# Attention and FFN in chunks of 512 tokens in place of 384

## The chip, the core and the metric

The kernel runs on one core of one Trainium2 chip. A core has five engines that run their own instruction streams in order: PE (TensorE, matrix multiply), DVE (VectorE), ACT (ScalarE), POOL (GpSimd) and SP (SyncE, which here only issues DMAs). They meet at semaphores. PE writes its results to PSUM, eight banks of 512 fp32 columns by 128 partitions; everything else lies in SBUF or in DRAM.

The metric is device time in microseconds. The kernel before takes 1013.74 us, the median of three runs (1013.64 to 1013.81).

## The reference

Windowed causal attention on 8 batches, 8 heads, 576 tokens and head size 64, then a feed-forward net with a rational function between its two products:

```python
scores = (1 / sqrt(64)) * q @ k.T              # window of 64: 0 <= i - j < 64
attn   = softmax(where(mask, scores, -1e9))
x      = (attn @ v)                            # to 4608 tokens x 512
h = x @ w_in                                   # 512 -> 2048
P = a[0] + a[1]*h + a[2]*h**2 + a[3]*h**3
Q = 1 + abs(b[0])*abs(h) + abs(b[1])*h**2
out = (P / (Q + 1e-6)) @ w_out                 # 2048 -> 512
```

## The kernel before

**Tiling.** The 4608 tokens are cut into 12 chunks of CH = 384. A chunk's attention is done in four *units*, one per pair of heads (`unit_load`, `unit_scores`, `unit_transpose`, `unit_av`). A unit leaves x transposed, 128 channels by CH tokens, split into a high part `xh` and a low part `xl`. The FFN goes through 16 tiles of 128 hidden channels; a *step* is one chunk and one such tile. `ffn1(c, i)` is 12 matmuls (four channel blocks, three products of high and low parts) into one bank `h` of CH columns, and then the rational function on ACT, DVE and POOL, which leaves `gh` and `gl`. `ffn2(s)` multiplies these with a tile of w_out: three matmuls of 512 columns for each 128 tokens, added up over a chunk's 16 steps in one output bank per 128 tokens (`o0` to `o2`).

**The rational function.** ACT reads h three times as absolute value and as two linear terms (L265 to L267); DVE continues the numerator (L268, L269); POOL multiplies u by |h| (L270); ACT takes logarithm and exponential of that (L273, L274), which together are the reciprocal; DVE forms gh and gl (L275 to L278). POOL stands between L267 and L273, and DVE behind L274.

**The attention unit.** PE writes the scores to the two banks `ps_s`; DVE adds the mask and takes the row maximum (L211, L214; in chunks 1 and 2 PE adds the mask, and only the maximum is left, L207); ACT takes exponentials with row sums (L221, L218); DVE makes reciprocals (L223, L224); POOL multiplies (L225; DVE in chunk 0); PE transposes into the same two banks (L232); ACT copies to `pT` (L234); PE multiplies with v into the bank `ps_x` (L243); ACT and DVE split that into xh and xl (L248, L249).

**Weights.** All weights stay in SBUF in a high and a low part. They arrive as 64-bit numbers and are decoded in 32 tiles: ACT (L124, L132), POOL (L127) and DVE (L128, L129, L133).

**Order.** `phases` lists the steps: chunks 0 and 1 go through the first eight hidden tiles, then both through the last eight, and then every chunk through all 16. So weights of the second half are needed only from step 16. Chunk 0's partial sums are put aside in SBUF between its two halves. FFN2 lags LAG = 3 steps behind FFN1 in the text of the program; the units of the next chunk begin AHEAD = 3 steps before the current chunk does. The text's order is not the engines' order: a scheduler with a model of the durations of its own places each engine's instructions when the program is built, within what data, buffers and banks allow. What buffers allow is set by the pools: PSUM has two banks for h, two for ps_s, one for ps_x and three for o.

Of the kernel before, what the change touches and what calls it, by code (L numbers as in the profile page):

```python
# [30 lines left out]
def swa_rational_ffn(ctx: ExitStack, tc: tile.TileContext, qT, kT, v, w_in, w_out, a, b, out):  # L31
# [71 lines left out]

    wi_h = const.tile([P, NCC, DFF], F32R, name="wi_h")
    wi_l = const.tile([P, NCC, DFF], F32R, name="wi_l")
    wo_h = const.tile([P, NF, DO], F32R, name="wo_h")
    wo_l = const.tile([P, NF, DO], F32R, name="wo_l")
# [45 lines left out]
    def unit_load(c, hp):  # L153
        q = kv.tile([P, TC, WIN], F32, name="q")
        kt = kv.tile([P, TC + 1, WIN], F32, name="kt")
        vt = kv.tile([P, TC, P], F32, name="vt")
# [20 lines left out]

        m0 = None if first is None else MASKS[first]
        live[c, hp] = dict(q=q, kt=kt, vt=vt, kw=kw, vw=vw, m0=m0)

    def unit_scores(c, hp):
        u = live[c, hp]

        ps = ps_a.tile([P, 2, 512], F32, name="ps_s", bufs=1)
# [9 lines left out]
        for p in range(PR):  # L194
            for z in range(2):
                for e in range(2):
# [8 lines left out]
        if on_pe:
# [3 lines left out]
        else:  # L209
# [4 lines left out]
            nc.vector.tensor_reduce(out=nmx, in_=sm, axis=AX.X, op=ALU.max, negate=True)  # L214
        sums = att.tile([P, NR], F32, name="sums")
        for j in range(NR):
# [3 lines left out]
            else:  # L220
                nc.scalar.activation(sm[:, j, :], sm[:, j, :], AF.Exp, bias=nmx[:, j:j + 1], accum_out=sums[:, j:j + 1])  # L221
# [6 lines left out]
    def unit_transpose(c, hp):  # L228
        u = live[c, hp]
        ps = ps_a.tile([P, 2, 512], F32, name="ps_s", bufs=1)  # L230
        for j in range(2 * PR):
            nc.tensor.transpose(ps[:, j // PR, (j % PR) * P:(j % PR + 1) * P], u["sm"][:, j, :], ident)  # L232
# [1 line left out]
        nc.scalar.copy(out=pT, in_=ps[:, :, 0:PR * P])  # L234
# [18 lines left out]
    def ffn1(c, i):  # L253
        h = ps_h.tile([P, CH], F32, name="h")
        n = 0
        for cc in range(NCC):
            for w, x in ((wi_h, xl), (wi_h, xh), (wi_l, xh)):
                nc.tensor.matmul(h, w[:, cc, i * P:(i + 1) * P], x[c, cc], start=n == 0, stop=n == 3 * NCC - 1)  # L258
                n += 1
# [28 lines left out]
    def ffn2(s):  # L288
# [3 lines left out]
        if first:  # L292
            acc[c] = [ps_o.tile([P, DO], F32, name=f"o{t}") for t in range(NTS)]
        gh, gl = gs.pop((c, i))
        for t in range(NTS):
            ts = slice(t * P, (t + 1) * P)
            for n, (g, w) in enumerate(((gl, wo_h), (gh, wo_l), (gh, wo_h))):
                nc.tensor.matmul(acc[c][t], g[:, ts], w[:, i, :], start=first and n == 0, stop=last and n == 2)  # L298
        if not last:
            return  # L300
        o = acc.pop(c)
        if c == 0 and c not in part:
# [4 lines left out]
        for t in range(NTS):
            ob = part[0][:, t, :] if s == total - 1 else stage.tile([P, DO], F32, name="ob", tag="w_st", bufs=3)
            if c in part:
                nc.vector.tensor_tensor(out=ob, in0=o[t], in1=part[c][:, t, :], op=ALU.add)  # L310
            else:
                nc.scalar.copy(out=ob, in_=o[t])
# [96 lines left out]
```

## Time and profile before

| | |
|---|---|
| median of three runs | 1013.74 us |
| the profiled execution (known by its span) | 1014.7 us |
| busy in the span: PE, DVE, ACT, POOL | 954.8, 825.9, 725.1, 324.9 us |
| matmuls of FFN1 (L258), 384 columns | 3 x 768 |
| matmuls of FFN2 (L298), 512 columns | 3 x 576 |
| mean granted clock of PE | 0.971 of full speed |

A row of a timeline has the start in us from the span's start, the duration, engine, line, operation, output and inputs, shapes and count, and in brackets how long the engine had been idle and what ended that. A matmul's duration is longer than the distance to the next one, since matmuls overlap; what one costs PE is the distance. A row of the groups has, behind the shapes, count, busy time in us, mean ns of one, and the idle time before them with what ended it. PE stands for matmuls, PEld for loads of the stationary operand, which overlap.

### The profile page before, as it was taken

How to read it: one execution, taken by the hardware profiler on the slowest of the kernel's cores; microseconds unless marked ns; L12 is line 12 of the kernel's file. 1: busy time of each engine (PE TensorE's matmuls, PEld its weight loads, DVE VectorE, ACT ScalarE, POOL GpSimd, SP SyncE). 2: the span in 40 equal slices, each digit the busy share in tenths (PEclk: the TensorE clock that was granted, in tenths of full speed). 3: DMA queues.
4: the chain of work that ended last, by engine and by line, in shares of the span. 5: the costliest groups of instructions: out<-in, count | busy, mean ns of one | idle time of the engine just before them, and what ended most of it. 6: DMA issues, size and time to landing. Idle time of an engine off the chain costs nothing.

```text
span 1014.7 us, 18277 instructions
## 1 busy us (share of the span) xinstructions
PE 954.8 (94%) x6640; PEld 844.8 (83%) x6640; DVE 825.9 (81%) x1539; ACT 725.1 (71%) x1735; POOL 324.9 (32%) x283
## 2 busy tenths in 40 slices
PE   3688578999999999999999999999999999999997
PEld 2576367989898888898888888888988988988996
DVE  7899788878888788788788787787787888787885
ACT  5777666667676777877777777777777777777664
POOL 4566544223332222223223223223223223222221
PEclk9679789999999999999999999999999999999999
DMA  7634630021211211210211211110121111100000
GB/s 239 221 110 138 207 98 16 1 77 29 90 31 31 83 42 34 88 37 29 76 46 31 67 58 34 64 61 29 61 61 31 62 63 35 64 17 1 32 1 31
DMA packets 37817, 64.09 MB, mean 63 GB/s; under 512 B 4448, under 2 KB 24928, under 8 KB 37728
## 3 DMA queue, kind: packets, MB, share of 16 engines
q1 hardware_dynamic: 37728, 62.93, 19.4%
q8 instruction: 52, 0.85, 0.4%
q14 instruction: 37, 0.30, 0.1%
HBM read 53.48 MB, written 9.44 MB: 62 GB/s over the span
## 4 chain that ended last, share of the span: by engine, by line
PE 84%; DVE 10%; ACT 3%; issue 2%; POOL 1%; DMA 1%; SPq 0%; POOLq 0%; DVEq 0%
PE h L258 38%; PE o L298 37%; PE ps_x L243 3%; PE ps_s L200 3%; PE ps_s L232 3%; DVE w_c L128 2%; POOL w_st L127 1%; DVE w_c L129 1%; DVE wo_l L133 1%; DVE num L277 1%; DVE u L276 1%; DVE wi_l L133 1%; DVE gh L275 1%; DMA w_st<-w_in 1%; ACT w_c L124 0%
## 5 line engine op out<-in xcount | busy, mean ns | idle before, releaser
L270 POOL TENSOR_TENSOR u<-u,ah 128x384 f32<-128x384 f32 x192 | 198.2, 1033 | 383.3 <-ACT u L267 343.7
L258 PE MATMUL h<-xl,wi_h 128*128 128x384 f32 x768 | 267.5, 348 | 20.3 <-DVE num L269 18.6
L258 PE MATMUL h<-xh,wi_h 128*128 128x384 f32 x768 | 262.7, 342 | 0.0
L258 PE MATMUL h<-xh,wi_l 128*128 128x384 f32 x768 | 262.5, 342 | 0.0
L298 PE MATMUL o<-wo_h,gl 128*128 128x512 f32 x576 | 233.5, 405 | 7.2 <-DVE gl L278 7.2
L298 PE MATMUL o<-wo_h,gh 128*128 128x512 f32 x576 | 228.3, 396 | 0.0
L298 PE MATMUL o<-wo_l,gh 128*128 128x512 f32 x576 | 227.0, 394 | 0.0
L268 DVE TENSOR_TENSOR num<-num,h 128x384 f32<-128x384 f32 x192 | 106.2, 554 | 111.9 <-ACT num L266 111.5
L265 ACT ACTIVATE ah<-h 128x384 f32<-128x384 f32 x192 | 94.5, 492 | 124.1 <-PE h L258 84.9
L258 PEld LDWEIGHTS h<-xl,wi_h 128*128 128x128 f32 x768 | 147.3, 192 | 27.8 <-DVE num L269 20.7
L258 PEld LDWEIGHTS h<-xh,wi_h 128*128 128x128 f32 x768 | 147.4, 192 | 4.8
L225 POOL TENSOR_TENSOR sm<-sm,rs 128x768 f32<-128x768 f32 x44 | 68.4, 1555 | 253.2 <-DVE rs L224 250.5
L258 PEld LDWEIGHTS h<-xh,wi_l 128*128 128x128 f32 x768 | 147.0, 191 | 0.6 <-issue 0.2
L275 DVE SCALAR_TENSOR_TENSOR gh<-num,a_sb,ah 128x384 fp32r<-128x384 f32 x192 | 119.3, 633 | 28.4 <-ACT ah L274 28.3
L298 PEld LDWEIGHTS o<-wo_h,gl 128*128 128x128 f32 x576 | 109.0, 189 | 33.7 <-DVE gl L278 8.8
L267 ACT ACTIVATE u<-ah,b_sb 128x384 f32<-128x384 f32 x192 | 135.6, 707 | 0.0
L221 ACT ACTIVATE sm<-sm,nmx 128x128 f32<-128x128 f32 x240 | 93.3, 390 | 57.4 <-DVE nmx L214 57.4
L298 PEld LDWEIGHTS o<-wo_h,gh 128*128 128x128 f32 x576 | 109.3, 190 | 25.2
L266 ACT ACTIVATE num<-h,a_sb 128x384 f32<-128x384 f32 x192 | 128.3, 668 | 0.0
L298 PEld LDWEIGHTS o<-wo_l,gh 128*128 128x128 f32 x576 | 109.2, 190 | 18.5
L269 DVE SCALAR_TENSOR_TENSOR num<-num,a_sb,h 128x384 f32<-128x384 f32 x192 | 117.7, 614 | 6.1
L277 DVE SCALAR_TENSOR_TENSOR num<-num,a_sb,u 128x384 f32<-128x384 f32 x192 | 116.7, 622 | 0.4
(52 smaller groups left out, 1139.2 us busy)
## 6 DMA issues: line engine op xcount, KB each, us to landing
out<-ob SPq DMA_DIRECT2D x33, 256.0 KB, 2.5
w_st<-w_in SPq DMA_DIRECT2D x16, 512.0 KB, 3.7
w_st<-w_out SPq DMA_DIRECT2D x16, 512.0 KB, 4.2
q<-qT SPq DMA_DIRECT2D x32, 192.0 KB, 3.2
vt<-v SPq DMA_DIRECT2D x16, 384.0 KB, 3.1
vt<-v SPq DMA_DIRECT2D x16, 320.0 KB, 3.0
kt<-kT SPq DMA_DIRECT2D x16, 224.0 KB, 3.6
kt<-kT SPq DMA_DIRECT2D x16, 192.0 KB, 3.4
```

The source lines that it names most:

```text
L221: nc.scalar.activation(sm[:, j, :], sm[:, j, :], AF.Exp, bias=nmx[:, j:j + 1], accum_out=sums[:, j:j + 1])
L225: (nc.vector if c < 1 else nc.gpsimd).tensor_tensor(out=sm, in0=sm, in1=rs.unsqueeze(2).broadcast_to([P, NR, P]), op=ALU.mult)
L258: nc.tensor.matmul(h, w[:, cc, i * P:(i + 1) * P], x[c, cc], start=n == 0, stop=n == 3 * NCC - 1)
L265: nc.scalar.activation(ah, h, AF.Abs)
L266: nc.scalar.activation(num, h, AF.Identity, scale=a_sb[:, 3:4], bias=a_sb[:, 2:3])
L267: nc.scalar.activation(u, ah, AF.Identity, scale=b_sb[:, 1:2], bias=b_sb[:, 0:1])
L268: nc.vector.tensor_tensor(out=num, in0=num, in1=h, op=ALU.mult)
L269: nc.vector.scalar_tensor_tensor(out=num, in0=num, scalar=a_sb[:, 1:2], in1=h, op0=ALU.add, op1=ALU.mult)
L270: nc.gpsimd.tensor_tensor(out=u, in0=u, in1=ah, op=ALU.mult)
L275: nc.vector.scalar_tensor_tensor(out=gh, in0=num, scalar=a_sb[:, 0:1], in1=ah, op0=ALU.add, op1=ALU.mult)
L277: nc.vector.scalar_tensor_tensor(out=num, in0=num, scalar=a_sb[:, 0:1], in1=u, op0=ALU.add, op1=ALU.subtract)
L298: nc.tensor.matmul(acc[c][t], g[:, ts], w[:, i, :], start=first and n == 0, stop=last and n == 2)
```

## The change

A chunk has 512 tokens, so there are nine. FFN1's matmuls and everything on h are 512 columns wide; a unit's scores, transposes and copies have eight blocks of 128 in place of six. An output chunk has four blocks of 128 tokens, held as two tiles of two banks each (`o0`, `o1`). To make room in PSUM, AV's result `ps_x` loses its own bank and takes turns with h in the two banks of `ps_h`; the scores of chunk 0 use the output banks. In SBUF, FFN2 lags two steps, the attention pools have one buffer, q and v of later chunks share the staging buffers of the weights, chunk 0's partial sums go to DRAM and come back, and the buffers of the attention of chunks 0 and 1 are given up at step SWITCH = 7 to the weights of the last eight tiles. The cut diff:

```diff
-CH = 384
+CH = 512
 TC = CH // WIN
 PR = TC // 2
 AHEAD = 3
-LAG = 3
+SWITCH = 7
+LAG = 2
...
-    kv = ctx.enter_context(tc.tile_pool(name="kv", bufs=2))
-    att = ctx.enter_context(tc.tile_pool(name="att", bufs=2))
+    kv = ctx.enter_context(tc.tile_pool(name="kv", bufs=1))
+    att = ctx.enter_context(tc.tile_pool(name="att", bufs=1))
...
+    early = ExitStack()
+    ekv = early.enter_context(tc.tile_pool(name="ekv", bufs=4))
+    eatt = early.enter_context(tc.tile_pool(name="eatt", bufs=2))
     ps_h = ctx.enter_context(tc.tile_pool(name="ps_h", bufs=2, space=bass.MemoryType.PSUM))
-    ps_a = ctx.enter_context(tc.tile_pool(name="ps_a", bufs=3, space=bass.MemoryType.PSUM))
+    ps_a = ctx.enter_context(tc.tile_pool(name="ps_a", bufs=1, space=bass.MemoryType.PSUM))
     ps_o = ctx.enter_context(tc.tile_pool(name="ps_o", bufs=1, space=bass.MemoryType.PSUM))
...
+    def weights(pool, tiles):
+        for i in tiles:
+            for d, n in (wi_h, "wi_h"), (wi_l, "wi_l"):
+                d[i] = pool.tile([P, NCC, P], F32R, name=f"{n}{i}")
+            for d, n in (wo_h, "wo_h"), (wo_l, "wo_l"):
+                d[i] = pool.tile([P, DO], F32R, name=f"{n}{i}")
+
+    weights(const, range(H))
...
+        if c < 2:
+            q = ekv.tile([P, TC, WIN], F32, name="q")
+            kt = ekv.tile([P, TC + 1, WIN], F32, name="kt")
+            vt = ekv.tile([P, TC - 1, P], F32, name="vt")
+        else:
+            q = stage.tile([P, TC, WIN], F32, name="q", tag="w_c")
+            kt = kv.tile([P, TC + 2, WIN], F32, name="kt")
+            vt = stage.tile([P, TC, P], F32, name="vt", tag="w_st", bufs=3)
...
+    def scores_bank(c, hp):
+        if c:
+            return ps_a.tile([P, 2, 512], F32, name="ps_s")
+        return ps_o.tile([P, 2, DO], F32, name="ps_s", tag=f"o{hp % 2}")
...
-        ps = ps_a.tile([P, TC, WIN], F32, name="ps_x", bufs=1)
+        ps = ps_h.tile([P, TC, WIN], F32, name="ps_x", tag="h")
...
-            acc[c] = [ps_o.tile([P, DO], F32, name=f"o{t}") for t in range(NTS)]
+            pair = [ps_o.tile([P, 2, DO], F32, name=f"o{t}") for t in range(NTS // 2)]
+            acc[c] = [pair[t // 2][:, t % 2, :] for t in range(NTS)]
...
-            part[c] = const.tile([P, NTS, DO], F32, name="part")
+            part[c] = []
             for t in range(NTS):
-                nc.scalar.copy(out=part[c][:, t, :], in_=o[t])
+                ob = stage.tile([P, DO], F32, name="ob", tag="w_st", bufs=3)
+                nc.scalar.copy(out=ob, in_=o[t])
+                part[c].append(tc.dram_tile([P, DO], F32, name=f"part{t}"))
+                nc.sync.dma_start(out=part[c][t], in_=ob)
             return
...
             if c in part:
-                nc.vector.tensor_tensor(out=ob, in0=o[t], in1=part[c][:, t, :], op=ALU.add)
+                nc.sync.dma_start(out=ob, in_=part[c][t])
+                nc.vector.tensor_tensor(out=ob, in0=o[t], in1=ob, op=ALU.add)
...
     for s in range(total + LAG):
+        if s == SWITCH:
+            early.close()
+            weights(ctx.enter_context(tc.tile_pool(name="late", bufs=1, reuse_waits="tile")), range(H, NF))
```

The scheduler makes other orders of it. Lines move too: L265 to L278 are L286 to L299 in the change, L221, L223, L224 are L242, L244, L245, L232, L234, L243 are L253, L255, L264, and L298 is L319. Three places from the middle of the program follow, one unit of a late chunk each.

PE before, where a unit's transposes (`ps_s<-ident,sm`) stand; xl and xh are FFN1's inputs, o is an output bank:

```order
L298 MATMUL o_2698<-wo_h,gh 128x512
L232 MATMUL ps_s<-ident,sm 128x128 x6
L258 MATMUL h<-xl_2428,wi_h 128x384
L258 MATMUL h<-xh_2427,wi_h 128x384
L258 MATMUL h<-xh_2427,wi_l 128x384
L258 MATMUL h<-xl_2645,wi_h 128x384
```

PE now, at the same place:

```order
L319 MATMUL o_5021<-wo_h_1187,gh 128x512
L253 MATMUL ps_s<-ident,sm 128x128 x8
L264 MATMUL ps_x<-pT,vt 64x64 x16
L279 MATMUL h<-xl_3771,wi_h_1193 128x512
L279 MATMUL h<-xh_3770,wi_h_1193 128x512
L279 MATMUL h<-xh_3770,wi_l_1194 128x512
```

Before, 24 matmuls of FFN1 (two steps) stand between the transposes and AV (`ps_x<-pT,vt`), which needs the copy pT of their result; now AV stands right behind them. It is so in 27 of the 28 units of chunks 2 to 8.

ACT before, from one unit's copy pT to the next step pair (ah, num and u belong to the step whose h they read):

```order
L234 COPY pT_3967<-ps_s_3960 128x768
L265 ACTIVATE ah_4086<-h_4073 128x384
L266 ACTIVATE num_4088<-h_4073,a_sb_87 128x384
L267 ACTIVATE u_4087<-ah_4086,b_sb_89 128x384
L265 ACTIVATE ah_4160<-h_4147 128x384
L266 ACTIVATE num_4162<-h_4147,a_sb_87 128x384
L267 ACTIVATE u_4161<-ah_4160,b_sb_89 128x384
L273 ACTIVATE ah_4086<-u_4087 128x384
L248 CAST xh3_3982<-ps_x_3969 128x384
L274 ACTIVATE ah_4086<-ah_4086 128x384
L273 ACTIVATE ah_4160<-u_4161 128x384
L274 ACTIVATE ah_4160<-ah_4160 128x384
```

ACT now, from one unit's copy on:

```order
L255 COPY pT_4497<-ps_s_4488 128x1024
L269 CAST xh3_4516<-ps_x_4499 128x512
L286 ACTIVATE ah_4545<-h_4532 128x512
L287 ACTIVATE num_4547<-h_4532,a_sb_93 128x512
L288 ACTIVATE u_4546<-ah_4545,b_sb_95 128x512
L294 ACTIVATE ah_4545<-u_4546 128x512
L295 ACTIVATE ah_4545<-ah_4545 128x512
L286 ACTIVATE ah_4587<-h_4574 128x512
L287 ACTIVATE num_4589<-h_4574,a_sb_93 128x512
L288 ACTIVATE u_4588<-ah_4587,b_sb_95 128x512
L294 ACTIVATE ah_4587<-u_4588 128x512
L295 ACTIVATE ah_4587<-ah_4587 128x512
```

Before, the first three operations of two steps stand together, and the logarithms behind both; now each step is finished before the next is opened. A third step of the same form follows, then the unit's eight exponentials, a fourth step and the next copy pT. At a chunk's end the four copies to the output buffers stand among these: two before the last operation of the step ahead of the eight exponentials, two around the start of the step behind them.

DVE before, where a unit's row sums (`sums`) stand against gl:

```order
L277 SCALAR_TENSOR_TENSOR num_4088<-num_4088,a_sb_87,u_4087 128x384
L277 SCALAR_TENSOR_TENSOR num_4162<-num_4162,a_sb_87,u_4161 128x384
L278 TENSOR_TENSOR gl_4090<-num_4088,ah_4086 128x384
L278 TENSOR_TENSOR gl_4164<-num_4162,ah_4160 128x384
L223 SCALAR_TENSOR_TENSOR sums_4127<-sums_4127,zero_126 128x6
L224 RECIPROCAL rs_4134<-sums_4127 128x6
```

DVE now, where the third step's gl is made:

```order
L296 SCALAR_TENSOR_TENSOR gh_4632<-num_4631,a_sb_93,ah_4629 128x512
L297 SCALAR_TENSOR_TENSOR u_4630<-u_4630,gh_4632 128x512
L244 SCALAR_TENSOR_TENSOR sums_4677<-sums_4677,zero_132 128x8
L298 SCALAR_TENSOR_TENSOR num_4631<-num_4631,a_sb_93,u_4630 128x512
L245 RECIPROCAL rs_4686<-sums_4677 128x8
L299 TENSOR_TENSOR gl_4633<-num_4631,ah_4629 128x512
```

The row sums, which need all eight exponentials, stood behind both gl; now they stand ahead of the last two operations that make one.

More of the change, by code (lines that the diff above doesn't have):

```diff
@@ L40, in swa_rational_ffn @@
     NCH = NTOK // CH
+    H = NF // 2
     NTS = CH // P
@@ L79, in make_mask @@
         nc.vector.tensor_copy(out=mask, in_=raw[:, 0:1, :].broadcast_to([P, NM, P]))
-        for j, half in FIRST.items():
+        for half, j in enumerate(KIND):
             hs = slice(half * 64, half * 64 + 64)
@@ L101, in swa_rational_ffn @@
     nc.vector.memset(zero, 0.0)
[L104 to L107, printed above, removed]
+    wi_h, wi_l, wo_h, wo_l = {}, {}, {}, {}
+    def weights(pool, tiles):
[5 more added lines that the diff above has]
+    weights(const, range(H))
     w_out_v = w_out.rearrange("(fc p) e -> p fc e", p=P)
@@ L135, in load_w_in @@
     def load_w_in(i):
-        sl = slice(i * P, (i + 1) * P)
-        decode(w_in[i], wi_h[:, :, sl], wi_l[:, :, sl])
+        decode(w_in[i], wi_h[i], wi_l[i])
     def load_w_out(i):
-        decode(w_out_v[:, i, :], wo_h[:, i, :], wo_l[:, i, :])
+        decode(w_out_v[:, i, :], wo_h[i], wo_l[i])
     xh, xl = {}, {}
@@ L153, in unit_load @@
     def unit_load(c, hp):
-        q = kv.tile([P, TC, WIN], F32, name="q")
-        kt = kv.tile([P, TC + 1, WIN], F32, name="kt")
-        vt = kv.tile([P, TC, P], F32, name="vt")
+        if c < 2:
[6 more added lines that the diff above has]
+            vt = stage.tile([P, TC, P], F32, name="vt", tag="w_st", bufs=3)
         kw, vw, first = [], [], None
@@ L176, in unit_load @@
             vb += nw
-        m0 = None if first is None else MASKS[first]
+        m0 = None if first is None else KIND[first % 2] - first // 2
         live[c, hp] = dict(q=q, kt=kt, vt=vt, kw=kw, vw=vw, m0=m0)
+    def scores_bank(c, hp):
+        if c:
+            return ps_a.tile([P, 2, 512], F32, name="ps_s")
+        return ps_o.tile([P, 2, DO], F32, name="ps_s", tag=f"o{hp % 2}")
     def unit_scores(c, hp):
         u = live[c, hp]
-        ps = ps_a.tile([P, 2, 512], F32, name="ps_s", bufs=1)
+        pool = eatt if c < 2 else att
+        ps = scores_bank(c, hp)
         m0 = u["m0"]
@@ L201, in unit_scores @@
                                      k[:, w:w + P], start=not on_pe, stop=not on_pe or p == PR - 1)
-        sm = att.tile([P, 2 * PR, P], F32, name="sm")
+        sm = pool.tile([P, 2 * PR, P], F32, name="sm")
         NR = 2 * PR
-        nmx = att.tile([P, NR], F32, name="nmx")
+        nmx = pool.tile([P, NR], F32, name="nmx")
         if on_pe:
@@ L214, in unit_scores @@
             nc.vector.tensor_reduce(out=nmx, in_=sm, axis=AX.X, op=ALU.max, negate=True)
-        sums = att.tile([P, NR], F32, name="sums")
+        sums = pool.tile([P, NR], F32, name="sums")
         for j in range(NR):
@@ L221, in unit_scores @@
                 nc.scalar.activation(sm[:, j, :], sm[:, j, :], AF.Exp, bias=nmx[:, j:j + 1], accum_out=sums[:, j:j + 1])
-        rs = att.tile([P, NR], F32, name="rs")
+        rs = pool.tile([P, NR], F32, name="rs")
         nc.vector.scalar_tensor_tensor(out=sums, in0=sums, scalar=1e-9, in1=zero, op0=ALU.add, op1=ALU.add)
@@ L229, in unit_transpose @@
         u = live[c, hp]
-        ps = ps_a.tile([P, 2, 512], F32, name="ps_s", bufs=1)
+        ps = ps_a.tile([P, 2, 512], F32, name="ps_s")
         for j in range(2 * PR):
             nc.tensor.transpose(ps[:, j // PR, (j % PR) * P:(j % PR + 1) * P], u["sm"][:, j, :], ident)
-        pT = att.tile([P, 2, PR * P], F32, name="pT", bufs=1)
+        pT = (eatt if c < 2 else att).tile([P, 2, PR * P], F32, name="pT")
         nc.scalar.copy(out=pT, in_=ps[:, :, 0:PR * P])
@@ L257, in ffn1 @@
             for w, x in ((wi_h, xl), (wi_h, xh), (wi_l, xh)):
-                nc.tensor.matmul(h, w[:, cc, i * P:(i + 1) * P], x[c, cc], start=n == 0, stop=n == 3 * NCC - 1)
+                nc.tensor.matmul(h, w[i][:, cc, :], x[c, cc], start=n == 0, stop=n == 3 * NCC - 1)
                 n += 1
@@ L297, in ffn2 @@
             for n, (g, w) in enumerate(((gl, wo_h), (gh, wo_l), (gh, wo_h))):
-                nc.tensor.matmul(acc[c][t], g[:, ts], w[:, i, :], start=first and n == 0, stop=last and n == 2)
+                nc.tensor.matmul(acc[c][t], g[:, ts], w[i], start=first and n == 0, stop=last and n == 2)
         if not last:
```

12 lines of the change are left out of this document (5 added, 7 removed).

## Prediction

> **What bounds the kernel now.** I read the page's head first, then the busy time by stretches of time, then the chain of work that ended last, then the timelines of the four engines over one attention unit.
>
> ```profile
> span 1014.7 us, 18277 instructions
> PE   3688578999999999999999999999999999999997
> 0.00:212.70 212.70, 158.63 (x1103) 135.49 (x1104) 184.15 (x310) 142.31 (x348) 101.69 (x79) 0.87 0.40 125
> 0.00:253.50 253.50, 199.43 (x1389) 171.52 (x1390) 215.84 (x372) 172.25 (x422) 112.90 (x89) 0.89 0.36 114
> 500.00:1000.00 500.00, 500.00 (x3447) 447.32 (x3446) 403.60 (x772) 364.50 (x858) 139.33 (x128) 1.00 0.13 42
> ```
>
> The columns of the stretches are length, busy PE, weight loads, DVE, ACT, POOL, granted clock, DMA share, GB/s. There are two regimes. From about 175 us on PE has no gap. Before that it is idle a quarter of the time, and DVE, busy 184.15 of the first 212.7 us, leads: it decodes 32 weight tiles there. The chain and PE's timeline show what PE spends per piece:
>
> ```profile
> 399.09 4.13 PE o L298 x18
> 403.87 4.24 PE h L258 x24
> 418.32 4.13 PE o L298 x18
> 422.28 0.82 PE L232 MATMUL ps_s<-ident,sm 128*128 128x128 f32 x6
> 422.86 0.42 PE L258 MATMUL h<-xl,wi_h 128*128 128x384 f32 x1
> 427.20 0.92 PE L243 MATMUL ps_x<-pT,vt 128*64 128x64 f32 x24
> 428.05 0.89 PE L200 MATMUL ps_s<-kt,q 64*64 64x128 f32 x24
> 428.87 0.50 PE L298 MATMUL o<-wo_h,gl 128*128 128x512 f32 x1
> ```
>
> A 512-column matmul takes 4.13/18 = 0.2294 us of PE, a 384-column one 4.24/24 = 0.1767. One unit adds 0.58 (transposes, 422.28 to 422.86), 0.85 (AV) and 0.82 (scores). The 19.23 us from 399.09 to 418.32 are four steps and one unit. The copy pT that AV needs lies under 24 FFN1 matmuls.
>
> **What PE saves.** FFN2 keeps 1728 matmuls of 512. FFN1 goes from 2304 x 0.1767 = 407.1 to 1728 x 0.2294 = 396.4 us: 10.7 less. A line through the two rows has 0.41 ns a column and 19 ns for each matmul whatever its width, and it is those that 576 fewer matmuls save. The Trainium skill ("TensorE: Matmul & The Clock Gate", section "Wait — 56ns, not 53.3ns?") puts the cost at N/2.4 GHz plus about 2.5 ns, by which the saving would be an estimated 1.5 us; the rows differ from it. Attention keeps its columns: 36 units of 4/3 the size for 48. Transposes, AV and scores become 0.77, 1.13 and 1.09 us a unit.
>
> **What the new order adds.** In the change AV follows its transposes directly in 27 of the 28 units of chunks 2 to 8, with nothing between them to cover pT. ACT finishes each step before it opens the next, so it sits through POOL's multiply. And c's gl stands behind the row sums of the exponentials on DVE. Durations for a walk through one unit:
>
> ```profile
> 418.35 0.49 ACT L265 ACTIVATE ah<-h 128x384 f32<-128x384 f32 x1
> 418.74 0.67 ACT L266 ACTIVATE num<-h,a_sb 128x384 f32<-128x384 f32 x1
> 419.30 0.71 ACT L267 ACTIVATE u<-ah,b_sb 128x384 f32<-128x384 f32 x1
> 421.14 0.53 ACT L273 ACTIVATE ah<-u 128x384 f32<-128x384 f32 x1 [0.16 <-POOL u L270]
> 421.69 0.53 ACT L274 ACTIVATE ah<-ah 128x384 f32<-128x384 f32 x1
> 423.14 0.80 ACT L234 COPY pT<-ps_s 128x768 f32<-128x768 f32 x1 [0.92 <-PE ps_s L232]
> 435.16 0.39 ACT L221 ACTIVATE sm<-sm,nmx 128x128 f32<-128x128 f32 x1
> 435.74 0.49 ACT L265 ACTIVATE ah<-h 128x384 f32<-128x384 f32 x1
> 436.58 1.47 POOL L225 TENSOR_TENSOR sm<-sm,rs 128x768 f32<-128x768 f32 x1 [6.52 <-DVE rs L224]
> 438.01 1.02 POOL L270 TENSOR_TENSOR u<-u,ah 128x384 f32<-128x384 f32 x1
> 432.23 0.95 DVE L214 TENSOR_REDUCE nmx<-sm 128x6 f32<-128x768 f32 x1
> 433.10 1.02 DVE L276 SCALAR_TENSOR_TENSOR u<-u,gh 128x384 f32<-128x384 f32 x2
> 434.03 1.14 DVE L277 SCALAR_TENSOR_TENSOR num<-num,a_sb,u 128x384 f32<-128x384 f32 x2
> L248 ACT CAST xh<-ps_x 128x384 fp32r<-128x384 f32 x48 | 22.7, 473 | 3.8 <-PE ps_x L243 3.0 <-PE h L258 0.8
> L312 ACT COPY ob<-o 128x512 f32<-128x512 f32 x30 | 16.4, 586 | 0.0
> L268 DVE TENSOR_TENSOR num<-num,h 128x384 f32<-128x384 f32 x192 | 106.2, 554 | 111.9 <-ACT num L266 111.5
> L310 DVE TENSOR_TENSOR ob<-o,part 128x512 f32<-128x512 f32 x3 | 2.1, 687 | 0.5 <-PE o L298 0.5
> ```
>
> 128 more columns cost ACT 586 - 473 = 0.11 us and DVE 687 - 554 = 0.13. No row has POOL's 512-column multiply: by the slope between its 384 and 768 columns it is 1.17, by proportion 1.36; I take 1.17, since both ends of that slope are measured. ACT's chain for a step, from start to start, is then 0.50 + 0.67 + 0.81, POOL 1.17 with 0.11 around it, 0.66 + 0.54: **4.46 us**. Eight exponentials take 7 x 0.39 + 0.58 = 3.3, pT 0.80 + 0.22 = 1.02. DVE's independent operations start every 0.60 to 0.66 us (0.47 and 0.53 in the rows, plus 0.13), the row maximum 1.14.
>
> The walk, t = 0 at AV, steps a to d, unhindered on PE: AV to 1.13, FFN1(a) to 3.88, FFN1(b) to 7.59, FFN1(c) to 12.85, most of FFN1(d) to 15.33, FFN2(a) to 18.08, rest of d to 18.77, FFN2(b) to 21.5, FFN2(c) to 24.3, transposes to 25.0. ACT starts a at 4.1 and ends a, b, c at 8.6, 13.0, 17.5, the exponentials at 20.8, d at about 26. DVE takes up gh of b at 13.1, and with two mask additions, the row maximum and c's first half before it, gl(b) is ready at 19.3: PE waits 0.6. c's gl, behind the row sums, is ready at 22.6: PE waits 0.5 more. Transposes then end at 26.2, pT begins 0.3 later and ends at 27.5, where AV begins: 1.4 of waiting. **A unit takes 27.5 instead of 25.0 us**, and 19.23 x 4/3 = 25.6 now. With POOL at 1.36 it would be 28.1; with only pT's wait 26.4.
>
> At a chunk's end four output copies (586 ns) enter ACT's chain: two ahead of c's last operation, two around the start of d. That delays gl and pT by about 1.6 us, at five places. The four stores and four loads of chunk 0's partial sums, the single buffer of kt, and AV in FFN1's banks I cost at nothing. The loads wait on SP for the scores of the unit before, with v's and q's loads and the stores queued behind them, but a whole unit (some 20 us of FFN work) lies over that; FFN1(b), which takes AV's bank, starts 3.7 us behind AV's end, and xh and xl need about 1.5. Without that cover each would cost a load or a cast, 1 to 4 us once or per unit. Behind the waiting AV stands FFN1(a) on PE, and for that ACT and DVE wait: so nothing of the 2.5 us is made up elsewhere.
>
> **The start.** Decoding does not grow with the chunk:
>
> ```profile
> L129 DVE SCALAR_TENSOR_TENSOR w_c<-w_st,w_c 128x512 uint32<-128x512 uint32 x32 | 26.0, 814 | 0.2
> L128 DVE SCALAR_TENSOR_TENSOR w_c<-w_c,w_st 128x512 uint32<-128x512 uint32 x32 | 25.0, 781 | 6.8 <-POOL w_st L127 6.6
> L133 DVE SCALAR_TENSOR_TENSOR wo_l<-w_c,wo_h 128x512 fp32r<-128x512 f32 x16 | 13.3, 833 | 0.4 <-ACT wo_h L132 0.4
> L133 DVE SCALAR_TENSOR_TENSOR wi_l<-w_c,wi_h 128x512 fp32r<-128x512 f32 x16 | 12.7, 791 | 1.9 <-ACT wi_h L132 1.9
> 212.70 1.02 DVE L278 TENSOR_TENSOR gl<-num,ah 128x384 fp32r<-128x384 f32 x2
> ```
>
> At 212.70 gl of step 23 stands. DVE's 184.15 us until then are 77.0 of decoding and 107 of the rest, which grows by 687/554 to 133: 210. At the same idle share (212.7/184.15) gl of step 23 comes at 243. From there to chunk 2 PE has seven blocks of FFN1 and 7.75 of FFN2 (12 matmuls, 2.753 each) = 41, four units of 3.0 = 12, and four waits for pT of 1.4 = 6: FFN1 of chunk 2 begins near **302 us**.
>
> **The sum.** From there on PE has 225 blocks at 2.753 = 620, 23 times transposes and AV (1.90) = 44, 24 scores (1.09) = 26: 690. Waits: 22 units x 2.5 = 55, five chunk ends x 1.6 = 8. The end of the program costs some 6 us, as it does now (a wait for the last gl, copies and stores). 302 + 690 + 63 + 6 = **1061** of span. The profiled execution's 1014.7 lies 1.0 above the median of the runs, 1013.74, so the time is 1060.
>
> **Rivals.**
> 1. Only pT's wait shows (1.4 a unit, nothing at FFN2 and the chunk ends): 63 becomes 31, the time 1028. For it: my gl's miss their place by 0.5 us, within what DVE's intervals are good for. I give it 0.17.
> 2. The clock falls in the gaps.
>
> ```profile
> 43.32 0.92 PE L243 MATMUL ps_x<-pT,vt 128*64 128x64 f32 x24 [0.89 <-ACT pT L234]
> 46.73 0.34 PE L258 MATMUL h<-xh,wi_l 128*128 128x384 f32 x1
> 65.31 0.55 PE L298 MATMUL o<-wo_h,gl 128*128 128x512 f32 x1 [2.00 <-DVE gl L278]
> 66.08 0.63 PE L298 MATMUL o<-wo_h,gh 128*128 128x512 f32 x1
> 66.51 0.63 PE L298 MATMUL o<-wo_h,gl 128*128 128x512 f32 x1
> ```
>
> After 2.00 us of idling FFN2's matmuls came every 0.43 us, nearly twice 0.2294, for nine matmuls: 1.8 us lost. After 0.89 with small matmuls around it (43.32) nothing fell. If every gap of 1.4 did it: 23 x 1.8 = 41, 1100. I give it 0.10. The same page of the Trainium skill ("Why this matters for your kernels") warns only of gaps above about 3 us; by that rule this rival would be worth nothing, but the row with 2.00 does not agree with so wide a limit.
> 3. Faster: the longer steps hide the decoding. The first 253.5 us hold 54 of idle PE, and 512 tokens give each tile more PE work to hide under. If DVE's idle share fell to nothing, gl of step 23 would come at 210, chunk 2 at 269, and with rival 1's waits the time is 995. It decides where the start is done before about 287. Against it: between decodings the order holds a stretch (steps 2 to 4) where ACT, POOL and PE take turns and DVE has no tile to decode. 0.08.
> 4. The late weights, which may be decoded only when chunk 1's attention is over, come late and FFN1 waits for them: up to 20 more, 1080. 0.05. That the change would not do what it says is excluded by its order: nine chunks, 512 columns.
>
> **How the numbers follow.** The forecast has 0.60. The range takes in rival 1 with a start ten early (1018) and, above, POOL's other bound (22 x 0.6 = 13), rival 4 and a clock that falls at some of the gaps: 1018 to 1094. About 0.2% is what a measurement of this kernel can tell from no change. Faster: rival 3, 0.08. Same: 0.04, between rivals 1 and 3. Slower: 0.88.
>
> **What would show it.** Right: PE's waits by line name AV for pT some 27 times at about 1.4 us, and FFN2 for gl at 0.5 to 1; ACT's Ln names POOL's multiply as what it waits for; units 27.5 us apart; PE's groups show FFN1 at 1728 matmuls. Wrong: no waits of AV (the walk is worthless), half-speed matmuls behind each AV (rival 2), or chunk 2 begun before 287 us (rival 3).

## The result and the profile after

The kernel with 512-token chunks takes **1123.18 us** (1122.38 to 1124.48) beside 1013.77 for the kernel before on the same chip: a ratio of **1.108** (95% interval 1.1064 to 1.1095), so 109 us slower. The forecast was 1060, and its range ended at 1094. The sign was right and the loss was more than twice the forecast one (46). Of one kernel below, the kernel before with AV in FFN1's banks, a fourth run took 1136.56 us at a granted clock of 0.844 in place of 0.98; its figures are those of the other three.

The head of the page of the changed kernel, PE's line of the 40 slices, and the group of the operation whose duration had to be estimated:

```profile
span 1122.7 us, 16288 instructions
PE   4657998698888999999989998999899998989997
L291 POOL TENSOR_TENSOR u<-u,ah 128x512 f32<-128x512 f32 x144 | 197.3, 1371 | 541.5 <-DVE num L289 303.6
```

Of the kernel before, every slice from the eighth to the last but one is full; now an 8 returns every few slices to the end. POOL's multiply takes 1.37 us: the proportion (1.36) was right, the slope (1.17) that I took was not.

The busy time by stretches of the changed kernel (columns as in the prediction):

```profile
100.00:160.00 60.00, 58.18 (x300) 46.30 (x299) 41.94 (x62) 37.74 (x75) 17.66 (x13) 0.97 0.14 45
160.00:240.00 80.00, 65.46 (x285) 50.73 (x284) 75.08 (x109) 49.52 (x93) 42.43 (x23) 0.94 0.31 97
322.00:1122.70 800.70, 741.31 (x4349) 568.97 (x4347) 554.77 (x818) 476.04 (x1004) 200.57 (x136) 0.99 0.13 40
500.00:900.00 400.00, 371.43 (x2268) 281.65 (x2267) 277.83 (x413) 243.11 (x537) 103.35 (x69) 0.99 0.15 43
```

From 500 to 900 us PE is idle for 28.6 of 400, where before it had no gap. Over the whole span it idles 131.5 us in place of 59.9. But idling is not all of the loss: PE is also *busy* longer for the same work, 991.2 us in the whole span beside 954.8 before. Its longest waits in total from 322 us on (engine, line and tile waited for: us in total, times, longest) are the two that the prediction named:

```profile
PE ps_x L264 <- ACT pT L255: 27.3, 22, 1.3
PE o L319 <- DVE gl L299: 24.8, 28, 3.1
```

Next, PE's timeline over one unit, cut to the places where it changes from one kind of work to another:

```profile
586.29 0.65 PE L221 MATMUL ps_s<-kt,q 64*64 64x128 f32 x10
586.87 0.50 PE L319 MATMUL o<-wo_h,gl 128*128 128x512 f32 x1
...
592.64 0.45 PE L221 MATMUL ps_s<-kt,q 64*64 64x128 f32 x8
593.02 0.50 PE L279 MATMUL h<-xl,wi_h 128*128 128x512 f32 x1
...
596.02 0.66 PE L221 MATMUL ps_s<-kt,q 64*64 64x128 f32 x14
596.62 0.50 PE L279 MATMUL h<-xl,wi_h 128*128 128x512 f32 x1
...
605.94 0.50 PE L319 MATMUL o<-wo_h,gl 128*128 128x512 f32 x1 [0.43 <-DVE gl L299]
608.86 1.03 PE L253 MATMUL ps_s<-ident,sm 128*128 128x128 f32 x8
611.16 1.03 PE L264 MATMUL ps_x<-pT,vt 128*64 128x64 f32 x28 [1.27 <-ACT pT L255]
```

Here is what the prediction put no price on. The scores of a unit, 32 small matmuls, come in **three pieces** (10, 8 and 14) spread over 10 us, with FFN work between them. They cost 0.58 + 0.38 + 0.60 = 1.56 us by the distances between starts, instead of 1.03 in one piece, and the FFN behind each piece starts again with a matmul of 0.33 instead of 0.23 us. The softmax can begin only when the last piece stands, at 596.6, and the transposes follow 12 us later, at 608.86. By then the FFN work of the unit is used up, so that FFN2 waits for a fresh gl at 605.94 and AV waits for pT at 611.16. The chain of work that ended last shows the queue of ACT and POOL at that place (its rows of 0.02 us called issue are left out):

```profile
605.45 2.19 POOL sm L246
607.64 1.26 POOL u L291
608.92 0.64 ACT ah L294
609.58 0.63 ACT ah L295
610.21 0.91 ACT pT L255
```

The copy pT stands in ACT's queue behind logarithm and exponential of a step, these behind POOL's multiply, and that behind POOL's multiply of the probabilities.

### The profile page after: what moved, and what is told of

Its sections match the earlier page's. It is cut to its first block, busy times and chain, and to the rows that moved or that the text cites. A ratio compares the mean times of both kernels' runs of the same rounds, so it can differ in the third digit from the quotient of the medians.

```text
span 1122.7 us, 16288 instructions
## 1 busy us (share of the span) xinstructions
PE 991.2 (88%) x6064; PEld 765.3 (68%) x6064; DVE 797.6 (71%) x1180; ACT 675.1 (60%) x1471; POOL 325.8 (29%) x223
## 4 chain that ended last, share of the span: by engine, by line
PE 31%; ACT 19%; DVE 14%; POOL 12%; issue 10%; DMA 2%; SPq 0%; POOLq 0%; DVEq 0%; ACTq 0%
PE h L279 16%; PE o L319 11%; POOL u L291 7%; ACT sm L242 5%; POOL sm L246 4%; DVE num L298 3%; ACT ah L294 3%; ACT ah L295 3%; PE ps_x L264 3%; DVE num L289 3%; ACT num L287 2%; DVE gh L296 2%; ACT pT L255 2%; DVE u L297 2%; ACT ah L286 2%
## 5 line engine op out<-in xcount | busy, mean ns | idle before, releaser
L291 POOL TENSOR_TENSOR u<-u,ah 128x512 f32<-128x512 f32 x144 | 197.3, 1371 | 541.5 <-DVE num L289 303.6
L319 PE MATMUL o<-wo_h,gl 128*128 128x512 f32 x576 | 240.9, 418 | 50.1 <-DVE gl L299 46.2
L279 PE MATMUL h<-xl,wi_h 128*128 128x512 f32 x576 | 236.6, 411 | 1.4 <-DVE num L290 1.4
L319 PE MATMUL o<-wo_l,gh 128*128 128x512 f32 x576 | 231.9, 403 | 0.0
L319 PE MATMUL o<-wo_h,gh 128*128 128x512 f32 x576 | 231.7, 402 | 0.0
L279 PE MATMUL h<-xh,wi_l 128*128 128x512 f32 x576 | 227.1, 394 | 0.0
L279 PE MATMUL h<-xh,wi_h 128*128 128x512 f32 x576 | 227.1, 394 | 0.0
L296 DVE SCALAR_TENSOR_TENSOR gh<-num,a_sb,ah 128x512 fp32r<-128x512 f32 x144 | 110.1, 765 | 149.1 <-ACT ah L295 148.8
L294 ACT ACTIVATE ah<-u 128x512 f32<-128x512 f32 x144 | 91.0, 632 | 188.6 <-POOL u L291 188.6
L319 PEld LDWEIGHTS o<-wo_h,gl 128*128 128x128 f32 x576 | 111.2, 193 | 101.1 <-DVE gl L299 61.8
L289 DVE TENSOR_TENSOR num<-num,h 128x512 f32<-128x512 f32 x144 | 98.4, 683 | 96.2 <-ACT num L287 96.0
L286 ACT ACTIVATE ah<-h 128x512 f32<-128x512 f32 x144 | 85.5, 593 | 130.7 <-PE h L279 101.3
L319 PEld LDWEIGHTS o<-wo_h,gh 128*128 128x128 f32 x576 | 111.7, 194 | 26.2
L319 PEld LDWEIGHTS o<-wo_l,gh 128*128 128x128 f32 x576 | 111.8, 194 | 22.2
L298 DVE SCALAR_TENSOR_TENSOR num<-num,a_sb,u 128x512 f32<-128x512 f32 x144 | 124.0, 861 | 1.7
L288 ACT ACTIVATE u<-ah,b_sb 128x512 f32<-128x512 f32 x144 | 117.3, 814 | 0.0
L287 ACT ACTIVATE num<-h,a_sb 128x512 f32<-128x512 f32 x144 | 111.5, 774 | 0.0
L290 DVE SCALAR_TENSOR_TENSOR num<-num,a_sb,h 128x512 f32<-128x512 f32 x144 | 107.1, 744 | 3.1
```

The source lines that it names most:

```text
L279: nc.tensor.matmul(h, w[i][:, cc, :], x[c, cc], start=n == 0, stop=n == 3 * NCC - 1)
L286: nc.scalar.activation(ah, h, AF.Abs)
L287: nc.scalar.activation(num, h, AF.Identity, scale=a_sb[:, 3:4], bias=a_sb[:, 2:3])
L288: nc.scalar.activation(u, ah, AF.Identity, scale=b_sb[:, 1:2], bias=b_sb[:, 0:1])
L289: nc.vector.tensor_tensor(out=num, in0=num, in1=h, op=ALU.mult)
L290: nc.vector.scalar_tensor_tensor(out=num, in0=num, scalar=a_sb[:, 1:2], in1=h, op0=ALU.add, op1=ALU.mult)
```

## The experiments

Two theories stood against each other. *Order*: what costs is the place of scores, transposes and AV on PE, so that another order with the same buffers and banks wins the loss back. *Resources*: AV in FFN1's banks, a lag of two or the slow POOL multiply costs of itself. A third matter is the start. All ratios are against the kernel before. Unless a paragraph says otherwise, the edit is made to the changed kernel.

**Own buffers for chunk 0's partial sums.** In the changed kernel they take the three buffers through which the weights arrive.

```diff
-                ob = stage.tile([P, DO], F32, name="ob", tag="w_st", bufs=3)
+                ob = stage.tile([P, DO], F32, name="pb", bufs=2)
```

> One edit: the copies of chunk 0's partial sums get two staging buffers of their own, so that they no longer take the three buffers in which weights arrive. In the changed kernel no DMA runs between about 100 and 147 us, the next weight load leaves at 149.71 us, behind the first three stores of partial sums, although the three loads before it were used up at 128 us, and from 160 to 240 us PE is idle for 14.5 us. Theory 'staging buffers': the next load leaves near 128 us, the idle PE of 160 to 240 us falls below 5, and the time is 1108 to 1113 us. Rival 'decoding work': DVE's and ACT's decoding itself sets the pace there, the idle time only moves to another place before 240 us, and the time stays within 3 us of 1123.

1120.4 us, 1.1051 (1.1034 to 1.1067). The idle time of PE from 160 to 240 us halves (14.5 to 7.4), that from 100 to 160 grows (1.8 to 6.2): a net 2.8 us. "Costed at nothing" was wrong, but by little.

**Scores whole.** Same banks, buffers and lag: in the later chunks the first score matmul of a unit keeps its low priority, and the others are issued behind it at a high one; the loop over p runs backwards.

```diff
-        for p in range(PR):
+        whole = ExitStack()
+        for p in reversed(range(PR)) if c > 2 else range(PR):
...
+                    mm1 = nc.tensor.matmul(ps[e * 64:e * 64 + 64, z, p * P:(p + 1) * P], u["q"][z * 64:z * 64 + 64, j, :],
...
+                    if c > 2 and (p, z, e) == (PR - 1, 0, 0):
+                        whole.enter_context(tc.issue_after(mm1.ins))
+                        whole.enter_context(tc.high_priority())
+        whole.close()
```

> One edit, in chunks 3 to 8: the matmuls of a unit's scores are queued as one piece and placed as soon as their inputs and banks are there, ahead of FFN work. Banks, buffers and LAG stay. By this order the scores of the next unit and one or two FFN1 tiles stand between a unit's transposes and its AV. Theory 'order': what a unit loses (1.5 us of waiting for pT, some 1.2 us for scores in three pieces and the matmuls that start again behind them) is a matter of the order, and goes: about 24 times 2 to 2.7 us, 1058 to 1075 us. Rival 'banks': with AV's result in FFN1's two banks PE finds no cover whatever the order; FFN1 waits for ACT and DVE to read a bank in place of AV waiting for pT, and the time is above 1100 us.

1031.71 us, 1.0184 (1.0167 to 1.0201): 91 of the 109 us are gone, more than the theory of the order had forecast. The middle stretch and the chain of this kernel (L222 is the scores, L258 the transposes, L269 AV, L284 FFN1, L324 FFN2):

```profile
500.00:900.00 400.00, 400.00 (x2631) 323.85 (x2629) 326.85 (x470) 278.29 (x605) 119.27 (x80) 1.00 0.15 48
```

```profile
540.14 1.03 PE ps_s L222 x32
541.18 1.08 PE ps_x L269 x32
542.26 5.82 PE o L324 x24
548.08 5.59 PE h L284 x24
553.67 2.81 PE o L324 x12
556.48 0.87 PE ps_s L258 x8
557.35 5.62 PE h L284 x24
```

PE has no gap. The scores are one piece and end 15 us ahead of the next transposes (541.18, 556.48) instead of 12, and between the transposes (556.48) and AV there are again 24 matmuls of FFN1, as in the kernel before. So neither the banks nor the lag force a wait; the order does.

**AV back out of FFN1's banks**, into the scores' bank.

```diff
-        ps = ps_h.tile([P, TC, WIN], F32, name="ps_x", tag="h")
+        ps = ps_a.tile([P, 2, 512], F32, name="ps_x", tag="ps_s")[:, 0, :].rearrange("p (t s) -> p t s", s=WIN)
```

> One edit: AV's result lies in the first of the two banks of the scores (free once pT is copied) in place of one of FFN1's two banks. By its order FFN blocks stand between transposes and AV in the late units, and the scores come in one piece. Theory 'banks': the waits for pT (38 us in all) go, and the pieces with them (about 1 us a unit): 1060 to 1075 us. Rival 'chain of ACT and POOL': PE then waits for gl instead, by about as much as it waited for pT, and the time is 1095 us or more.

1057.56 us, 1.0435 (1.0419 to 1.045): 66 less. The scores come in one piece here too. The waits of PE from 322 us on:

```profile
PE h L279 <- DVE num L290: 14.4, 4, 7.4
PE o L319 <- DVE gl L299: 6.6, 6, 2.0
PE ps_x L264 <- ACT pT L255: 3.3, 3, 1.1
```

**A lag of three steps.**

```diff
-LAG = 2
+LAG = 3
```

> One part of the change undone: LAG is 3 again (one more buffer each for gh and gl). Theory 'lag': FFN2's waits for gl (46 us in all, 39 times) fall to a few us, and the time to 1080 to 1090 us. Rival 'throughput of the chain': ACT, in line with POOL's 1.37 us multiply, works at its pace whatever the lag; PE's waits for gl or for a bank of h come back elsewhere, and the time stays above 1105 us.

1072.1 us, 1.0574 (1.0558 to 1.059): 51 less. Its waits from 322 us on:

```profile
PE ps_x L264 <- ACT pT L255: 20.6, 23, 1.1
PE o L319 <- DVE gl L299: 0.2, 1, 0.2
```

FFN2's waits for gl are gone there, 25 us, and AV waits 7 us less. Another 20 us are busy time (PE 971.3 beside 991.2): the scores come in 2.5 pieces on average, and fewer restarts follow.

**Scores whole from chunk 2 on, and the partial sums in buffers of the attention**; and the same with a lag of three.

```diff
-                ob = stage.tile([P, DO], F32, name="ob", tag="w_st", bufs=3)
+                ob = att.tile([P, DO], F32, name="pb", tag=("pT", "sm")[t % 2])
```

> The edits of scores_first (from chunk 2 on) and of pb_own together; the two buffers for the partial sums are those of pT and sm of late units, which are unused then. scores_first has PE idle for 13.3 us between 160 and 240 us and 10.6 between 240 and 322, and none from 360 us on. Theory 'order and start are separate': the gains add, 1031.7 less the 3 us of pb_own, 1026 to 1030 us. Rival 'the start is hidden by the late order in pb_own': with the late units mended the earlier weight loads are worth their whole hole, 1015 to 1022 us.

> The same and LAG 3. In scores_first all that is left of the waits for gl lies ahead of 322 us (23.4 us, 13 times). Theory 'order': with the scores early a lag of two is enough in the late chunks, so LAG 3 gives only what it takes from the start, 0 to 8 us: 1018 to 1030 us. Rival 'lag': the 51 us that LAG 3 alone gained are a gain of their own, and the time falls to 1000 us or less.

1028.77 us, 1.015 (1.0128 to 1.0172), the best kernel with 512 tokens, and 1030.9, 1.0166 (1.0146 to 1.0187). With the scores whole a longer lag has nothing left to win.

**The control: the scores edit on the kernel before.**

> A control: the kernel before, with the same edit of the scores (one piece, early) from chunk 2 on. Its PE has no idle time from 175 us on and its scores come in one piece already. Theory 'the change's order was at fault': nothing to gain, 1012 to 1016 us. Rival 'early scores are better everywhere': below 1009 us.

1013.72 us, 0.9987 (0.9975 to 1.0). The edit mends what the change broke; it is no gain of its own.

**AV in FFN1's banks alone, on the kernel before.**

```diff
-        ps = ps_a.tile([P, TC, WIN], F32, name="ps_x", bufs=1)
+        ps = ps_h.tile([P, TC, WIN], F32, name="ps_x", tag="h")
```

> One part of the change alone: the kernel before, with AV's result in FFN1's two banks. Theory 'order': the order made for it keeps FFN blocks between most transposes and AV, so it costs little, 1012 to 1022 us. Rival 'banks': PE waits for pT or for the reading of a bank in most of the 48 units, 0.5 to 1.4 us each: 1035 us or more.

1081.83 us, 1.066 (1.0632 to 1.0687). This one line, with 384 tokens, a lag of three and all the old buffers, costs 68 us, in the same form: PE is busy 983 us beside 954.8, and it waits where it didn't (the two largest over the span):

```profile
PE o L298 <- DVE gl L278: 28.1, 20, 4.7
PE ps_x L243 <- ACT pT L234: 16.8, 14, 2.9
```

The expectation that its order would stay regular failed: in the steady part the scores come in two pieces and cost 1.17 us a unit, where the kernel before has one of 0.82.

**AV a step later in the text.**

```diff
-                at(p + 1, unit_av, c, k)
+                at(p + 2, unit_av, c, k)
```

> One edit of the changed kernel: a unit's AV is written one step later in the program's text. By its order AV still stands directly behind the transposes and in FFN1's banks; but FFN1 and FFN2 alternate tile by tile, where in the changed kernel three FFN2 tiles in a row end each unit, the last of them only one step behind its FFN1, and the scores come in two pieces in place of three. It splits the loss of a unit: theory 'three FFN2 tiles in a row make gl late': the waits for gl of the late units (about 35 us in all) go, one piece and its restart go (0.3 us a unit), the waits for pT (1.5 us a unit) stay: 1075 to 1090 us. Rival 'gl is late because of the pace of ACT and POOL': gl's waits stay, 1110 us or more.

1068.22 us, 1.0531 (1.0515 to 1.0547): 55 less. AV still stands behind its transposes and waits (23 times, 28.8 us in all from 322 to 1000 us), but the scores come in two pieces, and FFN2 waits for gl once, 0.4 us.

**POOL's multiply on DVE.**

```diff
-        nc.gpsimd.tensor_tensor(out=u, in0=u, in1=ah, op=ALU.mult)
+        nc.vector.tensor_tensor(out=u, in0=u, in1=ah, op=ALU.mult)
```

> One edit of the changed kernel: the multiply of u by |h| (128x512, 1.37 us on POOL) runs on DVE (a product of that size takes 0.68 us there). Theory 'ACT's chain': ACT's waits for POOL (188.6 us, 119 times) shrink, gl comes about 0.7 us earlier in each step, the waits for gl (46.2 us) fall under 15, and the time is 1085 to 1100 us. Rival 'DVE': 144 times 0.68 us more on DVE in a row with the decoding of the weights and the late units' own work makes gl as late as before: 1115 us or more.

1124.24 us, 1.1088 (1.106 to 1.1115): no change. ACT's wait for this product falls from 188.6 to 118.2 us, and FFN2's for gl stays (46.2 and 41.8): DVE is busy 896.8 in place of 797.6 us, and gl is its own last product of a step. Taking POOL out of ACT's way doesn't move the end of the unit.

**A lag of two on the kernel before.** `LAG = 2` alone.

> One part of the change alone: the kernel before with LAG 2. Its order is regular, FFN1 tiles stand between transposes and AV, the scores come in one piece. Theory 'order': a lag of two is enough where the order is regular: 1010 to 1022 us. Rival 'lag': gl comes late in every step and FFN2 waits: 1040 us or more.

1015.96 us, 1.0023 (1.0008 to 1.0038): 2 us. Of itself the shorter lag costs next to nothing; undone in the changed kernel it saved 51. That fits an order without slack, to which the longer lag gave some.

The last three kernels ask what is left of the start. They are made from the best one (1028.77). The first also puts AV of chunk 2 alone into the scores' bank:

```diff
+        if c == 2:
+            ps = ps_a.tile([P, 2, 512], F32, name="ps_x", tag="ps_s")[:, 0, :].rearrange("p (t s) -> p t s", s=WIN)
+        else:
+            ps = ps_h.tile([P, TC, WIN], F32, name="ps_x", tag="h")
```

> The best version so far (sf_pb, 1028.8 us), and in chunk 2 alone AV's result lies in a bank of the scores. sf_pb has PE idle 8.8 us between 240 and 322 us, at chunk 2's units, whose AV stands directly behind the transposes. By its order FFN blocks stand between in two of the four units. Theory 'order': half of that goes, 1023 to 1027 us. Rival 'start bound by decoding and by gl': the idle time moves and the time stays within 2 us of 1028.8.

1042.55 us, 1.0278 (1.0254 to 1.0302): 14 worse. The scores of a unit now wait until AV's result is read out of their bank (1.4 us for xl at 307.75), and the transposes behind them wait for POOL's sm, 3.8 and 8.5 us at chunk 2.

The second moves AV a step later in the text, as above.

> sf_pb with AV written one step later in the text, the edit that took 55 us off the changed kernel. In sf_pb PE has no idle time from 360 us on, so nothing is left there; what the edit can still give lies in chunk 2's units, ahead of 322 us (PE idle 8.8 us between 240 and 322). Theory 'one loss': both edits mend the same loss, so together they give no more than 8 us beyond sf_pb, 1020 to 1030 us. Rival 'two losses': the gains of 91 and 55 us add at least in part, under 1010 us.

1030.41 us, 1.0159 (1.0142 to 1.0176): no gain on top of the scores.

The third tests the late weights. Their tiles are decoded as ever, but into spare buffers, and steps with a late tile read the weights of one of the first eight, so no FFN matmul waits for a late weight and no late weight for the early attention, whose buffers stay to the end. The output is that of the wrong weights.

```diff
+    for i in range(H, NF):
+        for d in wi_h, wi_l, wo_h, wo_l:
+            d[i] = d[i - H]
...
+        if i < H:
+            decode(w_in[i], wi_h[i], wi_l[i])
+        else:
+            decode(w_in[i], *(scrap.tile([P, NCC, P], F32R, name=n) for n in ("s_hi", "s_lo")))
```

> sf_pb without the wait of the late weights for the buffers of the early attention: the weights of the last eight tiles are loaded and decoded as always, but into spare tiles that nobody reads, and the matmuls of those tiles read the weights of the first eight in their place. All operations run, in the same sizes; the output is computed from the wrong weights. It measures what the late weights cost: both that they may be decoded only when chunk 1's attention is over (DVE is idle for 10 of the 20 us from 100 us on, PE for 6 between 160 and 240) and that FFN1 waits for them. Theory 'late weights': 1010 to 1020 us. Rival 'longer attention of the first chunk': what is lost against the kernel before is lost ahead of 100 us (47 us of idle PE there, 33.5 before) and stays, 1024 us or more.

1029.97 us, 1.0157 (1.0141 to 1.0172): no gain in the sum. At the start there is one: FFN1 of chunk 2 begins 3.9 us earlier (the best kernel, then this one), and PE idles 63.6 us in place of 68.6 up to 322.

```profile
313.48 0.50 PE L284 MATMUL h<-xl,wi_h 128*128 128x512 f32 x1
309.58 0.50 PE L294 MATMUL h<-xl,wi_h 128*128 128x512 f32 x1
```

Behind that a unit takes 25.72 us in place of 25.46, because FFN's matmuls come every 0.234 instead of 0.231 us; over 24 units that is some 6 us. Why they do, with the same sizes, stays open. So the late weights hold back the best kernel by some 4 us and not by the rest.

## Why the prediction was wrong

**The waits were right in kind, and too large for gl.** AV does wait for pT behind its transposes, in the steady part 1.24 us each time (27.3/22), where 1.4 was forecast. FFN2 does wait for gl, but of the walk's two waits, 0.6 for b's and 0.5 for c's, an ordinary unit shows one, of 0.43 to 0.51 us ahead of its third FFN2 block, as at 605.94. At four chunk ends 1.81 us come on top. The order of ACT (each step finished before the next is opened) and of DVE (row sums ahead of gl) does what the walk said.

**The step that failed is PE's work.** The span is 62 us longer than the forecast 1061: 20 of them arise in the start, and 42 from chunk 2 on. For that part the prediction gave PE 690 us of work (the row from 322 us on has it busy for 741), made of durations that the kernel before shows for unbroken stretches, and put AV in FFN1's banks at nothing; its walk prices the scores as one piece (1.09). The table is the mean over 16 units, in us, by the distances between the starts of PE's matmuls; waits and chunk ends are in it. The forecast's column is 27.5 with a quarter of a chunk end, 0.4.

| | forecast | after | lag of three | AV a step later | AV in the scores' bank | scores whole |
|---|---|---|---|---|---|---|
| FFN, with gl's waits | 23.5 | 24.64 | 23.09 | 22.65 | 22.75 | 22.56 |
| transposes, with pT's wait | 2.17 | 2.29 | 1.81 | 2.33 | 1.05 | 0.79 |
| AV | 1.13 | 1.08 | 1.08 | 1.08 | 1.26 | 1.08 |
| scores | 1.09 | 1.55 | 1.52 | 1.39 | 1.03 | 1.03 |
| pieces of the scores | 1 | 3 | 2.5 | 2 | 1 | 1 |
| unit | 27.9 | 29.55 | 27.50 | 27.44 | 26.09 | 25.46 |

- *After* is 1.65 us above the forecast in each unit. Scores in three pieces are 0.46 of it. The FFN matmuls beside a break, the first behind AV and the ones behind and ahead of each piece of the scores, take 0.33 and not 0.23: seven a unit, 0.70. Others behind a wait, or ahead of a stall too short to be listed, add 0.32, matmuls at half speed (23 in 16 units) 0.28, and the remaining ones, at 0.231 instead of 0.2294, 0.18. gl's waits are 1.12 by the distances, where 1.5 was forecast: 0.38 less. pT's wait adds 0.12, AV takes off 0.05.
- So PE's own time is some 1.9 above the forecast and the waits are 0.3 below it. With the scores whole four breaks a unit are left (0.39), and with 0.15 for the remaining matmuls FFN takes 22.56 instead of 96 x 0.2294 = 22.02.
- The prediction's rows held a sign of it: its pieces of four steps and a unit add up to 18.99 us, and from 399.09 to 418.32 the kernel before took 19.23.
- 24 units by 1.65 are 40 of the 42 us by which the stretch from chunk 2 to the end is longer than forecast (801 for 759).

**Chunk ends.** A unit with an end of a chunk took 32.3 us beside 28.75 for the others: 3.5 where 1.6 was forecast. That is in the mean above.

**The start.** FFN1 of chunk 2 begins at 321.72 and not at 302. Three rows of the changed kernel divide the 20 us:

```profile
254.71 0.69 DVE L299 TENSOR_TENSOR gl<-num,ah 128x512 fp32r<-128x512 f32 x1
308.35 0.65 PE L319 MATMUL o<-wo_h,gl 128*128 128x512 f32 x1 [2.55 <-DVE gl L299]
321.72 0.39 PE L279 MATMUL h<-xl,wi_h 128*128 128x512 f32 x1
```

gl of step 23 stands at 255.4 and not at 243. DVE's busy time up to there, 203, was forecast well (210); its idle time was not: 52 us instead of 33. The other 7 us lie between there and 321.72. The four units with pT's waits take 18.2 us there, as forecast (18), and the FFN matmuls are as many as counted. But the forecast had no wait for gl in this stretch, and there are three more, 4.5 us by the distances; eight matmuls behind the one at 308.35 run at half speed (1.6 us), and 14 beside a break or a wait cost 1.4. One hole in DVE's work is seen in SP's queue, where the stores of the partial sums hold the weights' buffers:

```profile
75.06 9.28 SPq L125 DMA_DIRECT2D w_st<-w_in  x3
...
146.96 1.81 SPq L329 DMA_DIRECT2D part<-ob  x3
149.71 0.33 SPq L125 DMA_DIRECT2D w_st<-w_in  x1
```

Between some 85 and 149.71 us no weight of the second half is loaded. This was the edit that I costed at nothing. It is real, but it is worth 2.8 us, since without it the wait only moves.

**The rivals.** gl's waits show beside pT's, so rival 1 is out. The clock did fall, in a few gaps only: from 322 us on about 29 matmuls ran at half speed, some 6 us in all, and not the 41 of rival 2. The late weights (rival 4) are worth some 4 us, by the last experiment, and not 20. The start didn't hide the decoding (rival 3): DVE idled more, not less. FFN1's saving is there: PE is busy 947.8 us with the scores whole, 7 less than before, where 10.7 was forecast.

**Where the cause lies.** It is shown that the order is enough: with banks, lag and buffers of the change and only the scores whole and early, the waits vanish in the late chunks and 91 us with them. What wholeness and what the higher priority is worth wasn't tried apart. It is shown too that AV in FFN1's banks brings this loss about: alone it costs 68 us on the kernel before, and undone in the changed kernel it saves 66. The four repairs save 91, 66, 55 and 51 us, more in sum than there was to lose. On top of the first the step later and the lag gain nothing; AV in the scores' bank was tried on top of it in chunk 2 alone, and lost. That fits one loss, an order without slack, which each of them loosens at another place. That AV's claim on a bank of h makes the scheduler's model place the scores as stop-gaps, in pieces, fits all of this, but which of its rules does so wasn't tried and stays open.

**What stays open.** With the order mended, 512 tokens still lose 15 us. The stretches of the best kernel (first two) and of the kernel before (last two):

```profile
100.00:160.00 60.00, 53.86 (x282) 41.95 (x281) 49.08 (x72) 40.77 (x80) 28.36 (x17) 0.96 0.22 68
160.00:240.00 80.00, 73.88 (x388) 58.23 (x387) 74.11 (x110) 52.79 (x107) 31.52 (x20) 0.96 0.25 74
```

```profile
100.00:160.00 60.00, 39.40 (x283) 32.64 (x282) 51.64 (x85) 39.23 (x96) 32.94 (x21) 0.81 0.41 129
160.00:240.00 80.00, 80.00 (x514) 70.54 (x513) 63.98 (x118) 53.37 (x120) 21.22 (x20) 0.99 0.12 38
```

At 160 us PE has done as much in both (busy 106.3 and 105.9 us), but DVE only 125 us in place of 141: it still has decoding before it (25 of the 32 weight tiles are begun, where the kernel before has begun all), and PE idles for 6 us from 160 to 240, where the kernel before has no gap. Most of DVE's lag arises in the first 100 us (busy 76.2 for 89.0), where the attention of a longer first chunk goes ahead. Whether that is the reason wasn't tried; the late weights' wait for buffers is some 4 of the 15 us.

## What to carry to other kernels

Take the price of small work from the way it will lie: the scores cut into three cost half as much again here (1.55 us for 1.03), each cut made the matmuls beside it dearer, and what depends on the whole group begins only behind the last piece. If two uses take turns in a bank, compare where *all* work of the unit ends up on the engine, not only the pair that shares the bank. And when several unrelated repairs each win back half of a loss but not their sum, look for one order that has run out of slack.

## What the hardware showed that was not expected

A gap in PE's work halved the speed of what followed, sometimes. Two chunk ends of the changed kernel, both after 1.81 us of waiting:

```profile
574.22 0.50 PE L319 MATMUL o<-wo_h,gl 128*128 128x512 f32 x1 [1.81 <-DVE gl L299]
574.79 0.63 PE L319 MATMUL o<-wo_h,gh 128*128 128x512 f32 x1
575.22 0.63 PE L319 MATMUL o<-wo_h,gl 128*128 128x512 f32 x1
```

```profile
811.36 0.50 PE L319 MATMUL o<-wo_h,gl 128*128 128x512 f32 x1 [1.81 <-DVE gl L299]
811.93 0.40 PE L319 MATMUL o<-wo_h,gh 128*128 128x512 f32 x1
812.16 0.39 PE L319 MATMUL o<-wo_h,gl 128*128 128x512 f32 x1
```

At 575 the matmuls come every 0.43 us, at 812 every 0.23; from 575 to 578 us the profile has a granted clock of 0.50. Of four such waits of 1.81 us three were followed by seven or eight matmuls at half speed; none of the waits of 1.10 to 1.45 us from 322 us on was, pT's among them. The Trainium skill ("TensorE: Matmul & The Clock Gate", section "Why this matters for your kernels") asks to avoid gaps of more than about 3 us; the rows here show the loss already behind 1.81 us, though not each time.
